# Q and K of batches 2 to 7 loaded four tokens to a partition, and the output weights' sums without one of their waits

## The chip, the cores and the metric

The kernel runs on one core of one Trainium2 chip. The metric is the time of one execution in device microseconds (us). Lower is better. A core has four compute engines, which run their own instruction streams and wait for each other by semaphores: TensorE (PE in the profile; its weight loads are PEld), VectorE (DVE), ScalarE (ACT) and GpSimd (POOL). SyncE (SP) issues transfers here and computes nothing; ACT and POOL issue some as well. All transfers are moved by the same 16 DMA engines of the core.

## What is computed

A block-causal attention over 8 batches of 8 heads, 576 tokens and 64 dimensions, and behind it a layer with a gate:

```
scores = q @ k.T / 8             # per batch and head; a block of 64 tokens sees itself and earlier blocks
attn   = softmax(scores)
x      = (attn @ v), heads side by side      # [4608, 512]
h      = x @ w_in                            # [4608, 2048]
out    = (h / (1 + exp(-beta * h))) @ w_out  # [4608, 512]
```

## The kernel before, in words

The work of attention is cut into 32 units: unit u is the pair of heads c = u % 4 of batch b = u // 4. The rest is cut into 9 chunks of 512 rows of x. All of it is one program on the five instruction streams.

**A unit.** Q and K of two heads are loaded in f32 to ST, cast to bf16 in QKn, transposed on TensorE (a product with the identity, identB) to PSUM, and copied from there to QKT, where a column is a token and the partitions hold the dimensions of two heads. From QKT come the scores (L823, matmuls of 64 rows, two side by side on the array), ScalarE's exponentials E (L844), zeros over what is masked (L850, L852), the product with V (L885), the division (L902, L909), and a transpose of the result (L928) to xT (L939, L941). V is loaded to Vs and cast to Vn (L588), one cast on POOL for a pair of heads.

**Two ways to load Q and K.** For batches 0 and 1 (QB = 2) a load (L710) takes 512 tokens of two heads with four tokens to a partition: 1 KB in a row from memory, 256 KB in all. The last 64 tokens of the batch's 8 heads (the tails) come by four loads of 64 KB (L674), are cast to QKt (L680) and transposed apart (L686, L696). A tile of a pair is four transposes for Q and four for K, each four to a PSUM tile of their own (L730). Their copy to QKT (L738) puts the tokens in order again: it reads the four transposed tiles in turn. For batches 2 to 7 a load (L753) takes all 576 tokens of four heads, 128 to a tile, 576 KB in packets of 256 bytes; four casts (L764) follow, 20 transposes for two units (L775) in PSUM tiles of 7, 7 and 6, and three copies (L785) in order, by VectorE, ScalarE and VectorE.

**A chunk.** For each of 16 pieces of the 2048 columns there are four matmuls (L1121), a tanh on ScalarE (L1131), and a product on VectorE (L1135) to gT. Chunk 0 then multiplies by w_out as it stands (L1157). Chunks 1 to 8 use a scheme of seven block products instead of eight (L1042); it needs sums and differences of quarters of w_out (L986, eight instructions on VectorE, written by `weights()`), and of gT (L1006). The sums TW are kept in OV, a buffer that at first holds V of batch 1; QKt lies in it too. In the kernel before, these sums wait for `wout` (the loads of w_out), for the users of what lay in OV, and for the last product of chunk 0 (`plain[-1:]`). The two that write into w_out itself wait for all of `plain` in any case.

**What sets the order.** A planner (`Plan.schedule`) goes through the operations with given durations, a model of two transfer rings, the number of buffers (slots) and eight PSUM banks. At each moment it starts on a free engine the ready operation with the lowest `prio`. What results is a fixed order for each engine, in which each instruction waits for semaphores on the chip. So an operation that is late on the chip holds all that stands behind it on its engine. `pr(u)` is the due number of a unit's work on TensorE. POOL's numbers are low for casts of Q and K, 4b + 0.5 for V's casts, and 4.6 for the loads of w_out parts 1 to 3 (L511, 512 KB each), which POOL issues; part 0 comes earlier. The loads of Q, K and V are issued by SP in a list's order: Q and K of the units, with the tails behind a batch's first pair, and V behind the fourth or second pair. Until the first 50 us of the plan are over, TensorE fills gaps with products that nobody reads (L447, L535).

Of the kernel before, what the change touches and what calls it, by code (L numbers as in the profile page):

```python
# [359 lines left out]
def bass_blockwise_causal_attn__then__act_swish_beta_kernel(  # L360
# [10 lines left out]
    with es:  # L371
# [1 line left out]
            return es.enter_context(nc.sbuf_tensor(name, shape, dt))  # L373

        NQ = 2
        QB, CAST = 2, "POOL"
        TURN = ((0, 7, "DVE"), (7, 14, "ACT"), (14, 20, "DVE"))
        NE = 3
        PARTS = [((0, 4, "SP", (4, 5, 0, 1, 2, 3)), (4, 8, "SP", range(2)), (4, 8, "POOL", (4, 5, 2, 3)))] + [((0, 8, "SP", range(6)),)] * 7
# [13 lines left out]
        TW = {k: OVh[:, k - 2] for k in (2, 3, 4)}  # L393
        SW = {k: OVh[:, k + 1] for k in (2, 3)}
        QKn = [sb(f"QKn{i}", [128, 2, 1280], bf16) for i in range(NQ)]
        QKt = OV[:, 0:256].bitcast(bf16).rearrange("p (w n) -> p w n", w=2)
        Vn = [sb(f"Vn{i}", [128, 5, 8, 66], bf16) for i in range(NQ)]
        QKT = [sb(f"QKT{i}", [128, 2, 1280], bf16) for i in range(3)]
        Ef = [sb(f"E{i}", [128, 3200], bf16) for i in range(NE)]
# [35 lines left out]
        def act_t(n, ptr=0):  # L435
            return 0.833 * n + 93 + 93 * ptr

        def dve_t(n):
            return (n + 125) / 0.96
# [174 lines left out]
        for u in range(NU):  # L614
# [8 lines left out]
            if b < QB:  # L623

                if c == 0:
                    quads = [(tn, tt_), (P.tile("QKn"), P.tile("QKT"))]
                    tq = P.tile("QKt")
                    early.append(tq)
                    tails = []
                    if b < 1:  # L630
                        tes_ = [P.tile("TT"), P.tile("TT")]
# [5 lines left out]
                        for a in range(2):  # L637
# [3 lines left out]
                            for w, src in enumerate((q, k)):  # L641
                                def fl(g, e, rows=rows, a=a, w=w, src=src):
                                    return [g.dma_start(STt[w][rows], src[0, 4 * a:4 * a + 4, 512:576].rearrange("h t d -> t h d"))]

                                def fn(g, e, rows=rows, w=w):
                                    y, x = QKt[rows, w, :], STt[w][rows].rearrange("p h d -> p (h d)")
                                    return g.activation(y, x, ACT.Copy) if e == "ACT" else g.tensor_copy(y, x)
# [4 lines left out]
                            def ft(g, e, pa=pa, rows=rows):  # L652
                                for i in range(4):
                                    z = g.transpose(PSb[:, pa.slot, 64 * i:64 * i + 64], QKt[rows, i // 2, 128 * (i % 2):128 * (i % 2) + 128], identB[rows, rows])
                                return z
# [46 lines left out]
                    tn, tt_ = quads[c // 2]  # L702
                    tail = tailc[c // 2]
                turned = []
                for w, (nm, src) in enumerate((("Q", q), ("K", k))):
                    ts, pt = P.tile("ST"), P.tile("P1")
                    early6.append(ts)

                    def fl(g, e, ts=ts, src=src, b=b, c=c):
                        return [g.dma_start(STm[ts.slot].rearrange("p h j d -> p h (j d)"),  # L710
                                            src[b, 2 * c:2 * c + 2, 0:512].rearrange("h (p j) d -> p h (j d)", j=4))]

                    o = ld[nm, u] = P.op("SP", 420 if b else 500, fl, tiles=[ts], xfer=750 if b else 820, prio=u, dma=["d_S", 0, 1])
                    o.pkt = 63.0

                    def fn(g, e, ts=ts, tn=tn, p=p, w=w):
                        return g.tensor_copy(QKn[tn.slot][:, p, 640 * w:640 * w + 512].rearrange("p (j h d) -> p j h d", j=4, h=2),
                                             STm[ts.slot].rearrange("p h j d -> p j h d"))

                    onp = u not in (0, 3) or w == 1  # L720
                    o = P.op("POOL" if onp else "DVE", 620 if onp else 430, fn, deps=[o], tiles=[ts, tn],
                             prio=-40 + 3 * u if onp else -1)
                    if u == 0 and w == 1:
                        for x in ones:
                            if x.dur < 160:
                                x.after = o if x.dur > 150 else None

                    def ft(g, e, tn=tn, pt=pt, p=p, w=w):
                        for i in range(4):
                            z = g.transpose(PSb[:, pt.slot, 128 * i:128 * i + 128],  # L730
                                            QKn[tn.slot][:, p, 640 * w + 128 * i:640 * w + 128 * i + 128], identB[:])
                        return z

                    o = P.op("PE", 4 * 56, ft, deps=[o, c4], tiles=[tn, pt, tt_], lat=4 * 56 + 170, mode="full",
                             prio=pr(u))

                    def fc(g, e, pt=pt, td=tt_, p=p, w=w):
                        return g.tensor_copy(QKT[td.slot][:, p, 640 * w:640 * w + 512].rearrange("c (p j) -> c p j", j=4),  # L738
                                             PSb[:, pt.slot, 0:512].rearrange("c (j p) -> c p j", j=4))

                    o.rest = 400.0 if b else 0.0

                    if u in (1, 3):
                        o.after = fqs[u - 1, 0]
                    turned.append(P.op("DVE", dve_t(512) + 30, fc, deps=[o], tiles=[pt, tt_], prio=-5 if b < 1 else .5))
                    turned[-1].after = last0["m"] if b else None
            elif p == 0:

                for w, (nm, src) in enumerate((("Q", q), ("K", k))):
                    ts = P.tile("S4")  # L750

                    def fl(g, e, ts=ts, src=src, b=b, c=c):
                        return [g.dma_start(STh[ts.slot], src[b, 2 * c:2 * c + 4].rearrange("h t d -> (h t) d").rearrange(  # L753
                            "(i p) d -> p i d", p=128))]

                    o = P.op("SP", QKI, fl, deps=[o for t in early6 for o in t.users] if b == QB else [],
                             tiles=[ts], xfer=QKX, prio=u, dma=["d_S4", 0, 1])
                    for i in range(2):
                        ld[nm, u + i] = o
                    for a in range(2):  # L760
                        def fn(g, e, ts=ts, tn=tn, a=a, w=w):
                            x = STh[ts.slot][:, 9 * a:9 * a + 5, :]
                            x = bass.AP(x.tensor, x.offset, [x.ap[0], [64, 5], [256, 2], [1, 64]])
                            return g.tensor_copy(QKn[tn.slot][:, a, 640 * w:640 * w + 640].rearrange("p (t h d) -> p t h d", t=5, h=2), x)  # L764

                        casts.append(P.op(CAST, 740, fn, deps=[o], tiles=[ts, tn], prio=u))

                turned = []
                for n0, n1, eng in TURN:
                    pt = P.tile("P1")  # L770

                    def ft(g, e, tn=tn, pt=pt, n0=n0, n1=n1):
                        x = QKn[tn.slot][:].rearrange("p a n -> p (a n)")
                        for i in range(n0, n1):
                            z = g.transpose(PSb[:, pt.slot, 128 * (i - n0):128 * (i - n0) + 128],  # L775
                                            x[:, 128 * i:128 * i + 128], identB[:])
                        return z

                    n = n1 - n0
                    o = P.op("PE", n * 56, ft, deps=casts, tiles=[tn, pt, tt_], lat=n * 56 + 170, mode="full", prio=pr(u))  # L780

                    def fc(g, e, td=tt_, pt=pt, n0=n0, n1=n1):
                        y = QKT[td.slot][:].rearrange("c a n -> c (a n)")[:, 128 * n0:128 * n1]
                        x = PSb[:, pt.slot, 0:128 * (n1 - n0)]
                        return g.activation(y, x, ACT.Copy) if e == "ACT" else g.tensor_copy(y, x)  # L785

                    turned.append(P.op(eng, act_t(128 * n) if eng == "ACT" else dve_t(128 * n), fc, deps=[o],
                                       tiles=[pt, tt_], prio=.5))
# [188 lines left out]
            return x[:, HJ * a:HJ * a + HJ, 256 * b:256 * b + 256]  # L977

        def weights():
            old = wout + plain[-1:] + [o for t in early for o in t.users]  # L980
            b = [quad(w_out, 0, 0), quad(w_out, 0, 1), quad(w_out, 1, 0), quad(w_out, 1, 1)]
            for k, o, x, y, op in ((3, TW[3], b[3], b[1], ALU.subtract), (2, TW[2], TW[3], b[0], ALU.add),
                                   (4, TW[4], b[2], TW[2], ALU.subtract), (1, b[1], b[1], b[0], ALU.subtract)):
                tw[k] = []
                for n in (slice(0, 4), slice(4, 8)):
                    z = P.op("DVE", dve_t(512), mk(lambda g, o=o, x=x, y=y, n=n, op=op: g.tensor_tensor(  # L986
                        o[:, n], x[:, n], y[:, n], op)), deps=old + (plain if k == 1 else []), prio=0.6)
                    z.same = [tw[q][len(tw[k])] for q in {2: [3], 4: [2]}.get(k, [])]
                    z.deps += z.same + ([tw[3][len(tw[k])]] if k == 1 else [])
                    tw[k].append(z)  # L990
# [260 lines left out]
```

## Time and profile before

| what | value |
|---|---|
| median of 10 runs | 352.73 us (351.41 to 354.05) |
| the profiled execution's own time | 352.78 us |
| its span in the profile | 350.7 us |
| TensorE's granted clock | 1.00 |
| busy: PE, DVE, ACT, POOL | 337.3, 234.5, 232.2, 83.7 us |
| products of x and w_in (L1121), one matmul of 512 columns | 576, 0.216 us apart |
| products with w_out in chunks 1 to 8 (L1042), of 256 columns | 1024, 0.109 us apart |
| transposes of Q and K in batches 2 to 7 (L775) | 240 |
| casts of Q and K in batches 2 to 7 (L764) | 48, 774 ns each |
| casts of V (L588) | 28, 770 ns each |
| loads of w_out (L511), issue to landing | 4, 11.2 us in the median |

The page's busy times count a matmul from its start to its end, while the next has already begun; so the distance of starts in the chain or the timeline, not the mean duration, says what one costs. Unit 8 is the first of batch 2. In the list of groups a line reads: line, engine, operation, out<-in, shapes, count | busy us, mean ns | idle us just before, and who ended it. In a timeline it reads: start, length, engine, line, operation, and in brackets the idle time before it with what ended it.

### The profile page before, as it was taken

What the parts mean: (1) busy time and instruction counts of PE and PEld (TensorE: products, weight loads), DVE (VectorE), ACT (ScalarE), POOL (GpSimd) and SP (SyncE); (2) the same over time, 40 slices, a digit from 0 to 9 for tenths busy, and PEclk for the clock granted to TensorE, in tenths of its full rate; (3) what the DMA queues carried; (4) which work ended last, traced back from release to release, by engine and by line L of the source; (5) the groups of instructions that cost most, each with busy time, mean ns of one, the idle gap of its engine ahead of it and who ended that gap; (6) DMA issues with size and microseconds to landing.
All of it is one profiled execution on the core that took longest, in us unless ns stands there. A gap on an engine that the chain in (4) does not pass through costs nothing.

```text
span 350.7 us, 8036 instructions
## 1 busy us (share of the span) xinstructions
PE 337.3 (96%) x3400; PEld 216.9 (62%) x3322; DVE 234.5 (67%) x488; ACT 232.2 (66%) x362; POOL 83.7 (24%) x131
## 2 busy tenths in 40 slices
PE   8999998999999999999999999999999999999996
PEld 2464465464656667666756676676676666666685
DVE  5667672378889476667857685849565777757742
ACT  3958952868686776876596758676688555545521
POOL 6952531547192034200630026000000000000000
DMA  8999998999999813981199020000000100020023
GB/s 233 244 253 235 204 211 153 255 239 204 203 229 238 153 62 79 227 163 62 33 224 210 3 92 0 32 32 33 30 32 2 62 30 33 0 92 30 0 93 120
DMA packets 113524, 42.30 MB, mean 121 GB/s; under 512 B 96576, under 2 KB 112976, under 8 KB 113488
## 3 DMA queue, kind: packets, MB, share of 16 engines
q1 hardware_dynamic: 98640, 28.78, 40.4%
q0 software_dynamic: 5568, 4.36, 7.9%
q10 hardware_dynamic: 9280, 8.65, 7.3%
q8 instruction: 26, 0.43, 0.5%
q14 instruction: 10, 0.08, 0.1%
HBM read 36.71 MB, written 9.44 MB: 132 GB/s over the span
## 4 chain that ended last, share of the span: by engine, by line
PE 76%; DMA 6%; ACT 5%; SPq 5%; DVE 4%; issue 2%; POOL 1%; POOLq 0%
PE PS L1121 28%; PE PS L1042 27%; PE PS L823 6%; PE PS L885 5%; DMA ST<-in_k_dram 4%; SPq L561 4%; PE PS L1157 3%; PE PS L775 3%; ACT E L844 2%; PE PS L928 2%; DVE gT L1135 2%; DMA ST<-in_q_dram 1%; ACT QKT L785 1%; ACT th L1131 1%; PE PS L447 1%
## 5 line engine op out<-in xcount | busy, mean ns | idle before, releaser
L1131 ACT ACTIVATE th<-PS,beta 128x512 f32<-128x512 f32 x144 | 96.4, 696 | 62.3 <-PE PS L1121 61.9
L1121 PE MATMUL PS<-xT,w_in 128*128 128x512 bf16 x534 | 130.0, 379 | 5.3 <-ACT xT L939 0.9
L1135 DVE SCALAR_TENSOR_TENSOR gT<-th,PS 128x512 f16<-128x512 f32 x144 | 95.7, 683 | 39.8 <-ACT th L1131 38.8
L844 ACT ACTIVATE E<-PS 128x1024 bf16<-128x1024 f32 x93 | 92.1, 1032 | 7.2 <-PE PS L823 6.3
L1121 PEld LDWEIGHTS PS<-xT,w_in 128*128 128x128 bf16 x576 | 53.1, 98 | 54.5 <-DVE gT L1135 2.5
L1042 PE MATMUL PS<-w_out,gT 128*128 128x256 f16 x512 | 63.4, 273 | 0.0
L1042 PEld LDWEIGHTS PS<-w_out,gT 128*128 128x128 f16 x512 | 48.6, 98 | 10.5 <-issue 0.6
L764 POOL CAST QKn<-ST 128x640 bf16<-128x640 f32 x48 | 37.1, 774 | 35.0 <-PE PS L775 21.8
L588 POOL CAST Vn<-Vs 128x640 bf16<-128x640 f32 (+1 forms) x28 | 21.5, 770 | 80.8 <-PE PS L885 66.2
L823 PE MATMUL PS<-QKT 64*64 64x64 bf16 (+4 forms) x328 | 34.0, 295 | 0.3 <-DVE QKT L738 0.3
L885 PEld LDWEIGHTS PS<-Vn,E 128*128 128x128 bf16 x930 | 30.9, 97 | 3.4 <-DVE E L852 0.3
L1042 PE MATMUL PS<-OV 128*128 128x256 f16 x256 | 32.7, 273 | 0.1
L885 PE MATMUL PS<-Vn,E 128*128 128x65 bf16 x930 | 32.0, 193 | 0.0
L1063 ACT ACTIVATE ost<-PS 128x512 f32<-128x512 f32 x32 | 19.6, 613 | 18.6 <-PE PS L1042 18.6
L823 PEld LDWEIGHTS PS<-QKT 64*128 64x128 bf16 (+1 forms) x328 | 13.2, 96 | 26.9 <-issue 8.2
L1042 PEld LDWEIGHTS PS<-OV 128*128 128x128 f16 x256 | 24.2, 98 | 5.9 <-issue 0.6
L909 DVE TENSOR_TENSOR xq<-PS,inv 128x640 bf16<-128x640 f32 x31 | 25.5, 822 | 0.8
L850 DVE MEMSET E<- 64x64 uint32 x62 | 6.9, 112 | 26.8 <-ACT E L844 24.9
L1006 DVE TENSOR_TENSOR OV<-gT 128x1024 f16<-128x1024 f16 x32 | 22.7, 715 | 0.7 <-PE PS L1042 0.4
L785 DVE COPY QKT<-PS 128x896 bf16<-128x896 bf16 (+1 forms) x24 | 13.7, 583 | 10.4 <-PE PS L775 10.2
L775 PE MATMUL PS<-identB,QKn 128*128 128x128 bf16 x240 | 17.1, 219 | 2.4 <-POOL QKn L764 1.4
L785 ACT ACTIVATE QKT<-PS 128x896 bf16<-128x896 bf16 x12 | 11.0, 917 | 10.9 <-PE PS L775 10.9
(80 smaller groups left out, 258.5 us busy)
## 6 DMA issues: line engine op xcount, KB each, us to landing
out_dram<-ost ACTq DMA_DIRECT2D x32, 256.0 KB, 2.3
ST<-in_q_dram SPq DMA_DIRECT2D x12, 576.0 KB, 5.5
ST<-in_k_dram SPq DMA_DIRECT2D x12, 576.0 KB, 7.6
Vs<-in_v_dram SPq DMA_DIRECT2D x24, 256.0 KB, 5.2
ST<-in_q_dram SPq DMA_DIRECT2D x8, 256.0 KB, 5.6
ST<-in_k_dram SPq DMA_DIRECT2D x8, 256.0 KB, 5.8
w_in<-in_moe_w_in_dram POOLq DMA_DIRECT2D x4, 512.0 KB, 11.6
w_out<-in_moe_w_out_dram POOLq DMA_DIRECT2D x4, 512.0 KB, 11.2
```

The source lines that it names most:

```text
L764: return g.tensor_copy(QKn[tn.slot][:, a, 640 * w:640 * w + 640].rearrange("p (t h d) -> p t h d", t=5, h=2), x)
L775: z = g.transpose(PSb[:, pt.slot, 128 * (i - n0):128 * (i - n0) + 128], x[:, 128 * i:128 * i + 128], identB[:])
L785: return g.activation(y, x, ACT.Copy) if e == "ACT" else g.tensor_copy(y, x)
L823: z = g.matmul(o, QKT[tqk.slot][r, uu % 2, 640 + 128 * t + y:640 + 128 * t + m + y], x)
L844: return g.activation(y, x, ACT.Exp, scale=0.125)
L885: z = g.matmul(o, eblk(te, t, i, h), Vn[Tv.slot][:, t, 2 * c + h, 0:65], start=(t == 0), stop=(t == i))
L909: return g.tensor_tensor(xq[xq_(tx)][:].rearrange("p i (h d) -> p h i d", h=2), both(pv, 0, 64), x, ALU.mult)
L1006: return P.op("DVE", dve_t(SZ * HC / 2), mk(lambda g: g.tensor_tensor(fo(), fx(), fy(), op)), deps=deps, tiles=tiles, prio=prio)
L1042: x = g.matmul(PS[:, pw.slot, HM * w:HM * w + HM], fa()[:, j, 128 * w:128 * w + 128], fb()[:, j, :], start=first and (pair or w == 0) and ...
L1121: z = g.matmul(PS[:, ph.slot, :], w_in[:, c, 128 * j:128 * j + 128], xT[:, c, row % RX:row % RX + RC], start=(c == 0), stop=(c == 3))
L1131: return g.activation(th[tt.slot][:], PS[:, ph.slot, :], ACT.Tanh, scale=beta[:, j:j + 1])
L1135: return g.scalar_tensor_tensor(out=gT[tg.slot][:, j, :], in0=th[tt.slot][:], scalar=1.0, in1=PS[:, ph.slot, :], op0=ALU.add, op1=ALU.mult)
```

## The change

QB becomes 8, so that batches 2 to 7 take the first of the two ways as well; the second has no users left. Within it, for batches 2 to 7 alone, the eight transposes of a unit (four of Q, four of K) share one PSUM tile of a whole bank (1024 elements in bf16) and wait for both casts; one copy takes all of them, on VectorE for even c and on ScalarE for odd c; both units of a pair are written together, as their scores are; and their due number is lower by 20. QKt becomes a buffer of its own outside OV, and its users leave the list that the sums wait for. The sums no longer wait for `plain[-1:]`.

```diff
-        QB, CAST = 2, "POOL"
+        QB, CAST = 8, "POOL"
...
-        QKt = OV[:, 0:256].bitcast(bf16).rearrange("p (w n) -> p w n", w=2)
+        QKt = sb("QKt", [128, 2, 256], bf16)
...
                     tq = P.tile("QKt")
-                    early.append(tq)
...
-                for w, (nm, src) in enumerate((("Q", q), ("K", k))):
-                    ts, pt = P.tile("ST"), P.tile("P1")
+                for cc in (c,) if b not in JOIN else (c, c + 1) if p == 0 else ():
+                    cast = []
+                    for w, (nm, src) in enumerate((("Q", q), ("K", k))):
+                        ts, pt = P.tile("ST"), P.tile("P1") if b < 2 or w < 1 else pt
...
+                        if b > 1:
+                            cast.append(o)
+                            if w < 1:
+                                continue
+                        else:
+                            cast = [o]
+
+                        def ft(g, e, tn=tn, pt=pt, p=cc % 2, ws=(w,) if b < 2 else (0, 1)):
+                            for w in ws:
+                                for i in range(4):
+                                    k = 128 * i + 512 * (w - ws[0])
+                                    z = g.transpose(PSb[:, pt.slot, k:k + 128],
+                                                    QKn[tn.slot][:, p, 640 * w + 128 * i:640 * w + 128 * i + 128], identB[:])
+                            return z
+
+                        nt = 4 if b < 2 else 8
+                        o = P.op("PE", nt * 56, ft, deps=[*cast, c4], tiles=[tn, pt, tt_], lat=nt * 56 + 170, mode="full",
+                                 prio=pr(4 * b + cc) - 20 * (b > 1))
...
+                        def fc(g, e, pt=pt, td=tt_, p=cc % 2, w=w, n=1 if b < 2 else 2):
+                            y = QKT[td.slot][:, p, :].rearrange("c (w x) -> c w x", w=2)[:, w + 1 - n:w + 1, 0:512].rearrange("c w (p j) -> c w p j", j=4)
+                            x = PSb[:, pt.slot, 0:512 * n].rearrange("c (w j p) -> c w p j", j=4, w=n)
+                            return g.activation(y, x, ACT.Copy) if e == "ACT" else g.tensor_copy(y, x)
+
+                        turned.append(P.op("ACT" if b > 1 and cc % 2 else "DVE", act_t(1024) if b > 1 and cc % 2 else dve_t(1024) + 150 if b > 1 else dve_t(512) + 30, fc, deps=[o], tiles=[pt, tt_], prio=-5 if b < 1 else .5))
...
-            old = wout + plain[-1:] + [o for t in early for o in t.users]
+            old = wout + [o for t in early for o in t.users]
```

In the changed kernel the lines are 11 further from the score products on: L834 for the scores, L844 becomes L855, L1132 and L1053 for the two products of a chunk, L1168 for chunk 0's product with w_out, L997 for the sums, L718 for the casts, L740 for the transposes, L754 for the copies, L679, L685 and L695 for the tails. The planner makes a new order for every engine. On POOL the loads of w_out parts 1 to 3 stood behind part 0 and the four casts of V of batch 1; now they stand behind part 0, four casts of Q and K and two of tails of batch 2 (units 8 and 9), and the four casts of V, in this order: part 0, Q 8, K 8, tail, V, tail, Q 9, V, K 9, V, V, parts 1 to 3. On VectorE six of the eight sums stand between the first and the second product to gT of chunk 1; before, all eight stood behind the sixteenth and last of these products.

## The prediction

> **What bounds the kernel now.** I read the page's head first, then the chain of waits in order of time, then the timelines of POOL, SP and PE around its largest wait, then the groups by line and form.
>
> ```profile
> span 350.7 us, 8036 instructions
> PE 337.3 (96%) x3400; PEld 216.9 (62%) x3322; DVE 234.5 (67%) x488; ACT 232.2 (66%) x362; POOL 83.7 (24%) x131
> PE 76%; DMA 6%; ACT 5%; SPq 5%; DVE 4%; issue 2%; POOL 1%; POOLq 0%
> ```
>
> TensorE is the bound: busy for 96% of the span, and 76% of the chain. The 6% and 5% of DMA and SP's queue lie in one place, which the chain in order of time shows:
>
> ```profile
> 33.80 1.69 SPq L561
> 35.52 0.89 SPq L564
> 37.76 15.78 DMA ST<-in_k_dram
> 53.59 0.73 POOL QKn L764
> 54.38 0.73 POOL QKn L764
> 55.15 0.95 PE PS L775 x14
> 56.11 0.86 PE PS L1157 x4
> ```
>
> So up to 55 us the kernel hangs on loads, and behind it on TensorE alone. From 64 us on I compared, in the trace, the starts of neighbouring matmuls with their columns at 2.4 per ns; what is lost to waits, switches of tile size aside, is some 4 us in 285. Whatever is saved on TensorE there shortens the run; whatever TensorE loses before 64 us lengthens it, for nothing behind can make it up.
>
> POOL's timeline has the instructions that the change rearranges (start, length, what, the wait before):
>
> ```profile
> 22.86 0.61 POOL L717 CAST QKn<-ST 128x512 bf16<-128x512 f32 x1 [0.59 <-DMA ST<-in_q_dram]
> 25.13 0.61 POOL L717 CAST QKn<-ST 128x512 bf16<-128x512 f32 x1 [1.66 <-DMA ST<-in_k_dram]
> ...
> 39.23 0.74 POOL L511 DMA_DIRECT2D w_out<-in_moe_w_out_dram  x1 [4.81 <-DMA OV<-in_v_dram]
> 39.97 3.08 POOL L588 CAST Vn<-OV 128x640 bf16<-128x640 f32 x4
> 42.99 2.22 POOL L511 DMA_DIRECT2D w_out<-in_moe_w_out_dram  x3
> 45.19 1.53 POOL L764 CAST QKn<-ST 128x640 bf16<-128x640 f32 x2
> 53.59 1.50 POOL L764 CAST QKn<-ST 128x640 bf16<-128x640 f32 x2 [6.87 <-DMA ST<-in_k_dram]
> ```
>
> POOL runs in order: what stands ahead of the three w_out issues delays them.
>
> **Part 1: tiles and transposes.** Batches 2 to 7 need 6 x (32 + 4) = 216 transposes instead of 240. Fourteen in a row take 0.80 us in the chain (at 94.56), 57 ns each, so 24 fewer are worth 24 x 0.057 = **1.4 us of TensorE**, all on the path. Scores, value products and both MLP products stay the same in number.
>
> **Part 2: evictions.** The groups by form give the rates:
>
> ```profile
> L738 DVE COPY QKT<-PS 128x512 bf16<-128x512 bf16 x16 | 10.9, 690 | 3.3 <-PE PS L730 3.1
> L785 DVE COPY QKT<-PS 128x896 bf16<-128x896 bf16 x12 | 7.4, 617 | 3.8 <-PE PS L775 3.8
> L785 ACT ACTIVATE QKT<-PS 128x896 bf16<-128x896 bf16 x12 | 11.0, 917 | 10.9 <-PE PS L775 10.9
> L941 DVE COPY xT<-PS 128x512 bf16<-128x512 bf16 x12 | 5.0, 418 | 0.5 <-PE PS L928 0.4
> ```
>
> The new copies read four tiles in turn (stride 128), as L738 does. Contiguous copies cost 0.52 ns an element more (617 against 418 for 384 more); the stride adds (690 - 418)/512 = 0.53. A strided one of 1024 is then 690 + 512 x 1.05 = 1.23 us (between 2 x 418 and 2 x 690). VectorE: 12 x 1.23 + 12 tails x 0.29 (L696) = 18.2 us, before 12 x 0.617 + 12 x 0.550 = 14.0. ScalarE: no row reads with a stride; 1024 elements take 1.03 us at L844, and with VectorE's ratio 690/418 it would be 1.70; I take 1.03, as the nearest row: 12.4 us for 11.0. Both engines are two thirds busy and the transposes come ahead of other PE work (due times 20 lower): cover of about 2.6 us, eight matmuls of L1042 and eight of L1121 (0.87 + 1.73), stands in the new order between a batch's last transposes and its first scores. Cost 0; without that cover the second copy would show, 1.23 less the 0.55 of before, in each of six batches: 4 us.
>
> The Trainium skill's page "VectorE: DVE Perf Modes", section "What auto-detection actually checks", speaks against this part: a 16-bit copy runs at two elements a cycle only with steps of one. The rows agree (690 against 418); by that rule too the copies lengthen and the sum stays, as long as VectorE has room.
>
> **Part 3: loads.** 24 loads of 576 KB become 48 of 256 KB and 24 of 64 KB; bytes are equal. Packets, by the trace: 55,296 of 256 B at 18 ns, against 12,288 of 1 KB at 47 ns and 6,144 of 256 B, over 16 engines 62 us against 43. From 120 us on DMA is mostly idle and this buys nothing; before that it frees the engines. POOL's casts go from 48 x 0.774 to 48 x 0.615 + 12 x 0.401, 37.1 to 34.3 us; it is idle for three quarters.
>
> **Part 4: POOL's queue, the deciding one.** The new order on POOL is: w_out part 0; casts Q8, K8; tail; V pair 4; tail; Q9; V 5; K9; V 6, V 7; then w_out parts 1 to 3 (Q8 is Q of unit 8, the first of batch 2). Before, these three were issued at 42.99 with only four V casts ahead. Now they stand behind K9's landing, and so do the V casts that the value products of units 5 and 6 need.
> When does K9 land? SP is free of batch 1's V at 37.1. Issues of 256 KB cost 0.51 us there and of 64 KB 0.65 (rows at 16 to 19 us), so Q8, K8, four tails, Q9, K9 go out at 37.1, 37.6, 38.1 to 40.1, 40.7 and 41.25. The nearest row is batch 1's second pair, also behind four tails and also with 512 KB weight loads beside it: issued at 16.43 and 17.08, cast at 22.86 and 25.13, 6.4 and 8.05 us later. By it K9 is cast at 49.3; from below, by the shortest landing of such a load (3.0 us), POOL's own work (39.97 + 4 x 0.66 + 2 x 0.45 + 2 x 0.81) lets it end at 45.1. I take 49.3. After 0.66 and two V casts (1.6) the weight parts are issued from 51.6 (from below 46.7).
> Landing: w_in part 0, issued at 13.92, had landed at 21.3, 7.4 us; w_out part 1 took 9.6 (42.99 to 52.6). The parts follow at 4.1 (w_in) or 3.4 us (w_out: 49.3, 52.6, 56.0, 59.4). The loads beside it are of 1 KB, as with w_in, so part 2 lands at 51.6 + 7.4 + 4.1 = **63.1** (57.5 to 65.3).
> In the new PE order the first product of chunk 1 stands behind four products with part 2: 63.1 + 0.9 = 64.0. Before it started at 62.64, with eight more output products done (1.73) and 0.2 of wait: the same work stood at 60.7. **TensorE loses 64.0 - 60.7 = 3.3 us.** At the upper end it is 5.5; at the lower nothing waits, and the gap before, 1.43 at 55.15 and 0.5 by the w_out wait, is won: -1.9. The loss is shared among waits for V 5, V 6 and parts 1 and 2, about 1.4, 0.6, 0.5 and 0.8 us.
>
> The page "DMA: Bandwidth & Descriptors", section "Latency and other measured facts", says that engines 7 and 15 are usually slower with GpSimd-issued transfers. The trace has such a laggard: 15 of 16 parts of the K load at 37.76 had landed by 47.6, the last at 53.5. Without a laggard K9 would come some 2 us earlier and the loss be near 1.3.
>
> **Part 5: weight sums.** Eight sums (L986, 0.69 to 1.2 us) ran from 93.7 to 106.8, behind the last L1157. Six now stand between the first and second gate product of chunk 1, 5 us of VectorE in one piece behind w_out part 3; behind them wait a PSUM bank and an eviction, and PE has output products and transposes in that time. PE's waits around the old place are 1.6 us. Either end is possible, -1.6 to +1.5. Together with the transposes' waits for banks (L775 on ScalarE, 1.8 us behind 75 us), of which batches with one burst may lose some, I take -0.5 for all behind 64 us.
>
> **Sum.** Against the profiled execution's 352.78 (span 350.7): 3.3 - 1.4 - 0.5 = +1.4, **354.2 us**. The median of the runs is 352.73, the same within 0.05.
>
> **Rivals.** (a) *Faster, about 350.4*: K9 lands by 46 and the weight parts before TensorE asks. For it: 1 KB packets move the same bytes in two thirds of the time, and only one weight part competes until then. Against: the row of batch 1. If nothing waits it is -1.9 - 1.4 - 0.5 = -3.8, 349.0; at the bound of 0.3% 351.7; I name the middle. It decides where part 2 lands before about 60.7. (b) *They cancel, 352.8*: part 2 lands near 61.7, and the loss is 1.9. (c) *Much slower, 358.2*: the strided evictions hold each batch's scores. At ScalarE's upper price, 1.70 for 1.03, it is 0.67 in each of six batches on top of the forecast, 4.0. For it: no row shows that copy. Against: PE's cover of 2.6 us, and both engines' idle third. It decides where the copies begin so late that the chain of two on one engine (2 x 1.23 + 0.29) outlasts the cover.
>
> **Numbers.** Forecast 0.45, (a) 0.27, (b) 0.18, (c) 0.10. A measurement of this kernel tells 0.3% (1.06 us) from no change, so (a) is faster, (b) the same, forecast and (c) slower: 0.27, 0.18, 0.55. The range goes from 349.8, within (a), to 357.4, which is the upper loss (5.5 - 1.4 + 0.5 behind 64 us); it leaves out the far part of (a) and (c). Since cases of both signs weigh, the forecast's own range is 353.9 to 357.4.
>
> **What would show it.** Right: POOL's wait for in_k_dram just ahead of the K cast before the last V casts of batch 1, w_out issued near 51, PE waits for w_out or POOL of 2 us or more between 45 and 66, chunk 1's first gate product near 64. Transposes 216, 57 ns apart. Wrong: w_out issued before 48, or chunk 1 starting before 61; a loss behind 70 us; PE waiting on QKT copies for more than 2 us in all.

## The result, and the profile after

The changed kernel takes 356.3 us (median of 18 runs) against 351.79 (63 runs of the kernel before beside it). The ratio is 1.0119, with a 95% interval from 1.010 to 1.0137: slower by 4.2 us, between 3.5 and 4.8. The profiled execution of the changed kernel took 355.98 us, with a span of 354.1; the one of the kernel before stood 1.0 us above its median in this comparison, so the two profiles lie closer together (3.4 us of span) than the kernels do.

The head of the page after:

```profile
span 354.1 us, 8097 instructions
PE 335.7 (95%) x3378; PEld 216.0 (61%) x3298; DVE 239.8 (68%) x488; ACT 234.4 (66%) x362; POOL 81.8 (23%) x143
PE 74%; DMA 12%; DVE 4%; ACT 4%; issue 3%; POOL 2%; SPq 0%; POOLq 0%
```

TensorE is busy for less time than before (335.7 for 337.3 us) in a longer span. DMA's share of the chain has doubled, and VectorE's stays at 4% though it now stands in other places. The chain in order of time shows which (start, length, what):

```profile
41.65 6.11 DMA ST<-in_q_dram
48.56 0.73 POOL Vn L588
50.02 0.73 POOL Vn L588
52.20 0.73 POOL w_out L511
52.93 15.06 DMA w_out<-in_moe_w_out_dram
68.02 1.76 DVE OV L997 x2
70.90 2.42 DVE OV L997 x3
73.97 0.79 PE PS L834 x12
74.76 0.97 PE PS L1168 x4
```

Before, the load of K for units 8 and 9 led to its casts and the transposes. Now the load of Q9 leads through its cast, K9's cast and three V casts (two of them are shown) to the w_out parts, w_out to the six weight sums, and the sums to a group of scores at 73.97. POOL's timeline has the first half of this:

```profile
40.29 0.74 POOL L511 DMA_DIRECT2D w_out<-in_moe_w_out_dram  x1 [4.49 <-DMA OV<-in_v_dram]
41.02 1.30 POOL L718 CAST QKn<-ST 128x512 bf16<-128x512 f32 x2
...
43.20 0.72 POOL L588 CAST Vn<-OV 128x640 bf16<-128x640 f32 x1
47.28 0.40 POOL L679 CAST QKt<-ST 128x256 bf16<-128x256 f32 x1 [3.36 <-DMA ST<-in_k_dram]
47.88 0.61 POOL L718 CAST QKn<-ST 128x512 bf16<-128x512 f32 x1 [0.20 <-DMA ST<-in_q_dram]
48.56 0.72 POOL L588 CAST Vn<-OV 128x640 bf16<-128x640 f32 x1
49.34 0.61 POOL L718 CAST QKn<-ST 128x512 bf16<-128x512 f32 x1
50.02 1.50 POOL L588 CAST Vn<-OV 128x640 bf16<-128x640 f32 x2
51.47 2.22 POOL L511 DMA_DIRECT2D w_out<-in_moe_w_out_dram  x3
```

The cast of V's second pair (48.56) could have run at 43.9, for its data had been there by 40.3, when the first instruction that waits for the loads of V of batch 1 (w_out part 0) ran. It stands behind the tail of K, which waited 3.36 us for its load. On TensorE's timeline this is the largest wait of the run behind 10 us:

```profile
45.59 1.07 PE L896 MATMUL PS<-Vn,E 128*128 128x65 bf16 x30
49.34 1.07 PE L896 MATMUL PS<-Vn,E 128*128 128x65 bf16 x30 [2.68 <-POOL Vn L588]
...
59.76 1.90 PE L1168 MATMUL PS<-w_out,gT 128*128 128x512 f16 x8 [0.56 <-DMA w_out<-in_moe_w_out_dram]
...
63.97 1.04 PE L1168 MATMUL PS<-w_out,gT 128*128 128x512 f16 x4 [1.50 <-DMA w_out<-in_moe_w_out_dram]
65.06 0.81 PE L1132 MATMUL PS<-xT,w_in 128*128 128x512 bf16 x3
...
73.97 0.79 PE L834 MATMUL PS<-QKT 64*128 64x320 bf16 x12 [1.38 <-DVE gT L1146]
```

Chunk 1's first gate product (65.06) had started at 62.64 before. The last line is a wait that Part 5 of the prediction named and then counted as covered: VectorE ran the six sums from 68.02 to 73.2 with nothing but two 0.11 us memsets between, the eviction of a gate product (L1146) stood behind them at 73.24, and the scores needed the PSUM bank that it frees.

The copies came out as estimated. By line and form (count | busy us, mean ns):

```profile
L754 DVE COPY QKT<-PS 128x1024 bf16<-128x1024 bf16 x12 | 14.5, 1218 | 1.2 <-PE PS L740 1.1
L754 ACT ACTIVATE QKT<-PS 128x1024 bf16<-128x1024 bf16 x12 | 12.3, 1024 | 7.3 <-PE PS L740 7.3
```

### The profile page after: what moved, and what is told of

Its sections match the earlier page's. It is cut to its first block, busy times and chain, and to the rows that moved or that the text cites. A ratio compares the mean times of both kernels' runs of the same rounds, so it can differ in the third digit from the quotient of the medians.

```text
span 354.1 us, 8097 instructions
## 1 busy us (share of the span) xinstructions
PE 335.7 (95%) x3378; PEld 216.0 (61%) x3298; DVE 239.8 (68%) x488; ACT 234.4 (66%) x362; POOL 81.8 (23%) x143
## 3 DMA queue, kind: packets, MB, share of 16 engines
q1 hardware_dynamic: 62544, 28.79, 32.5%
## 4 chain that ended last, share of the span: by engine, by line
PE 74%; DMA 12%; DVE 4%; ACT 4%; issue 3%; POOL 2%; SPq 0%; POOLq 0%
PE PS L1132 29%; PE PS L1053 26%; PE PS L896 6%; PE PS L834 6%; DMA ST<-in_k_dram 4%; DMA w_out<-in_moe_w_out_dram 4%; DMA ST<-in_q_dram 3%; PE PS L740 2%; ACT E L855 2%; PE PS L939 2%; DVE OV L997 1%; PE PS L1168 1%; DVE gT L1146 1%; POOL QKn L718 1%; ACT th L1142 1%
## 5 line engine op out<-in xcount | busy, mean ns | idle before, releaser
L1142 ACT ACTIVATE th<-PS,beta 128x512 f32<-128x512 f32 x144 | 97.4, 697 | 62.0 <-PE PS L1132 61.0
L1132 PE MATMUL PS<-xT,w_in 128*128 128x512 bf16 x536 | 130.6, 379 | 5.5 <-DVE gT L1146 1.8
L1146 DVE SCALAR_TENSOR_TENSOR gT<-th,PS 128x512 f16<-128x512 f32 x144 | 96.2, 683 | 43.2 <-ACT th L1142 42.7
L855 ACT ACTIVATE E<-PS 128x1024 bf16<-128x1024 f32 x93 | 91.9, 1025 | 11.0 <-PE PS L834 8.3
L1132 PEld LDWEIGHTS PS<-xT,w_in 128*128 128x128 bf16 x576 | 53.3, 98 | 55.6 <-DVE gT L1146 2.2
L1053 PE MATMUL PS<-w_out,gT 128*128 128x256 f16 x512 | 64.3, 273 | 0.0
L1053 PEld LDWEIGHTS PS<-w_out,gT 128*128 128x128 f16 x512 | 48.7, 98 | 13.6 <-issue 2.1
L718 POOL CAST QKn<-ST 128x512 bf16<-128x512 f32 x62 | 39.9, 644 | 25.0 <-DMA ST<-in_q_dram 10.6
L588 POOL CAST Vn<-Vs 128x640 bf16<-128x640 f32 (+1 forms) x28 | 20.4, 729 | 101.7 <-PE PS L896 94.3
L834 PE MATMUL PS<-QKT 64*64 64x64 bf16 (+4 forms) x328 | 34.0, 295 | 1.6 <-DVE gT L1146 1.4
L1053 PE MATMUL PS<-OV 128*128 128x256 f16 x256 | 32.7, 273 | 0.0
L834 PEld LDWEIGHTS PS<-QKT 64*128 64x128 bf16 (+1 forms) x328 | 13.2, 96 | 27.9 <-issue 11.0
L754 DVE COPY QKT<-PS 128x512 bf16<-128x512 bf16 (+1 forms) x28 | 25.5, 916 | 5.3 <-PE PS L740 4.9
L1053 PEld LDWEIGHTS PS<-OV 128*128 128x128 f16 x256 | 24.0, 98 | 4.7 <-issue 0.6
L740 PE MATMUL PS<-identB,QKn 128*128 128x128 bf16 x256 | 19.6, 222 | 2.5 <-ACT QKT L754 1.3
L740 PEld LDWEIGHTS PS<-identB,QKn 128*128 128x128 bf16 x256 | 15.9, 99 | 9.7 <-DVE QKn L718 2.9
```

The source lines that it names most:

```text
L740: z = g.transpose(PSb[:, pt.slot, k:k + 128], QKn[tn.slot][:, p, 640 * w + 128 * i:640 * w + 128 * i + 128], identB[:])
L834: z = g.matmul(o, QKT[tqk.slot][r, uu % 2, 640 + 128 * t + y:640 + 128 * t + m + y], x)
L855: return g.activation(y, x, ACT.Exp, scale=0.125)
L1053: x = g.matmul(PS[:, pw.slot, HM * w:HM * w + HM], fa()[:, j, 128 * w:128 * w + 128], fb()[:, j, :], start=first and (pair or w == 0) and ...
L1132: z = g.matmul(PS[:, ph.slot, :], w_in[:, c, 128 * j:128 * j + 128], xT[:, c, row % RX:row % RX + RC], start=(c == 0), stop=(c == 3))
L1142: return g.activation(th[tt.slot][:], PS[:, ph.slot, :], ACT.Tanh, scale=beta[:, j:j + 1])
```

## The experiments

Three theories stood at first. **W**: the loss is POOL's order, V casts and w_out behind the loads of batch 2. **S**: it is the six sums in one piece. **E**: it is the strided copies or the smaller loads. Each experiment was timed in five rounds beside the kernel before; a ratio is always to that kernel, with its 95% interval.

### POOL's order of before (e1_pool_order)

```diff
-                                 prio=-40 + 3 * (4 * b + cc) if onp else -1)
+                                 prio=(4 * b + cc if b > 1 else -40 + 3 * (4 * b + cc)) if onp else -1)
```

The tails' casts get `u + .5` for b > 1 in the same way.

> The changed kernel, but the POOL casts of batches 2 to 7 have the due number 4b + cc (their tails u + 0.5) as casts late in the queue had, so POOL's order around 40 us is the one of the kernel before: w_out part 0, four V casts of batch 1, w_out parts 1 to 3, then the casts Q8, K8, tails, Q9, K9. Tiles, transposes, copies, loads and the weights' sums stay as changed. Theory W (w_out and the V casts come late because they stand behind K9's landing): parts 1 to 3 are issued by 46 us, the waits of TensorE for the V cast (2.7 us) and for w_out (0.6 and 1.5 us) go, chunk 1's first gate product starts at 61 to 62.5 us, and the run is about 3 us shorter than the changed kernel, 352 to 353.5. Rival S (the burst of six weight sums on VectorE costs the time, the early waits are made up): 355.5 to 356.5. Rival E (strided copies or smaller loads cost it): 355.5 to 356.5, and the early waits move to the casts of batch 2.

Measured: 352.08 us, ratio 0.9999 (0.998 to 1.0019). The whole loss is gone. TensorE's timeline of this kernel:

```profile
54.51 1.04 PE L1168 MATMUL PS<-w_out,gT 128*128 128x512 f16 x4 [1.31 <-DMA w_out<-in_moe_w_out_dram]
...
62.55 0.81 PE L1132 MATMUL PS<-xT,w_in 128*128 128x512 bf16 x3
...
67.75 1.04 PE L1132 MATMUL PS<-xT,w_in 128*128 128x512 bf16 x4 [1.83 <-DVE gT L1146]
```

The V wait is gone and chunk 1 starts at 62.55. S and E fall as causes of the loss. (The planner orders TensorE anew as well, in this run and in all others: here 28 of chunk 0's 64 output products stand before chunk 1, in the changed kernel 24. So the comparison is with POOL's order and what the planner makes of it.) But a wait for w_out (1.31) and one for the sums' burst (1.83) stayed, against the expectation that the first would go; together they are more than the 1.9 us that the rest of the change was to win.

### The sums held again (e2_sums_held, e3_pool_order_sums_held, e4_before_sums_free)

```diff
-            old = wout + [o for t in early for o in t.users]
+            old = wout + plain[-1:] + [o for t in early for o in t.users]
```

e2 makes this edit in the changed kernel, e3 in e1. e4 does the reverse in the kernel before: QKt in a buffer of its own, and the sums free.

> The changed kernel with the weights' sums held again behind chunk 0's last product (plain[-1:] back in the list); POOL's order is the changed one. Theory W with the sums as a second, smaller term: only the wait of 1.4 to 1.5 us for a bank held by the burst at 73 us goes, the small waits around 96 to 107 us may return (up to 1 us): 354.5 to 356. Rival S (the sums are the whole loss): 352 to 353. The early waits of TensorE for the V cast and for w_out stay in either case, at 2.7 and 2 us.

> The changed kernel with both of the other two edits: POOL's order of before and the weights' sums held behind chunk 0's last product. What remains of the change is the tiles of four tokens, the 24 fewer transposes, the copies of 1024 and the loads of 256 KB. Theory W plus the sums: both losses go and the 1.4 us of transposes are won: 350.5 to 352, at or below the kernel before. Rival E (the strided copies or the smaller loads cost the time): 354 to 356.

> The kernel before with only the sums' part of the change: QKt in a buffer of its own, and the weights' sums not held behind chunk 0's last product nor behind the tails' users. POOL's order, tiles and loads are those of before. If the burst of six sums in one piece by itself holds a bank for TensorE, a wait of 1 to 1.5 us shows near 70 us and the small waits of before around 96 to 107 us (1 us in all) go: 352 to 353.5. Rival S (the sums are the whole loss): 355 to 356. If the sums find room in VectorE's idle time, as the prediction's -0.5 supposed: 351.5 to 352.5.

Measured: e2 359.63 us, 1.0182 (1.0139 to 1.0225); e3 353.16, 1.0027 (1.0002 to 1.0051); e4 352.19, 0.9996 (0.9976 to 1.0016). Theory S is wrong, and in e2 with the opposite sign: holding the sums costs the changed kernel 0.6% more. No theory had expected e2 above 356 us, nor e3 between 352 and 354. The 1.4 us wait at 73 us goes as expected, but the held sums then stand before the copies of the next tiles. TensorE's timeline of e2:

```profile
103.83 0.62 PE L740 MATMUL PS<-identB,QKn 128*128 128x128 bf16 x8 [0.51 <-ACT QKT L754]
104.92 0.40 PE L685 MATMUL PS<-identB,QKt 128*128 128x128 bf16 x4 [0.47 <-DVE QKT L754]
106.28 1.41 PE L1132 MATMUL PS<-xT,w_in 128*128 128x512 bf16 x3 [0.96 <-DVE QKT L695]
```

That is 1.9 us of waits for copies to QKT, and e3 has the same three (0.51, 0.53, 0.96). Most of the rest of e2's loss is half the granted clock for twice 3.4 us, 3.4 us of work in all. The last section shows the first stretch; the second begins at 106.3, behind the three waits above. The profile of the changed kernel has no such stretch. So each place of the sums has a price: about 1.4 to 1.8 us by the burst, about 2 us in the old place. In the kernel before (e4) freeing them changes nothing that can be measured, and its trace has no wait of more than 0.4 us for the burst.

### V casts or w_out? (e5_v_casts_first, e6_w_out_first)

W names two late things. e5 moves only batch 1's V casts ahead of Q8's cast, e6 only the w_out parts.

```diff
# e5
-                             prio=4 * b + 0.5 - (38.5 - 4.6 * (h0 > 0)) * (b < 1))
+                             prio=-17 if b == 1 else 4 * b + 0.5 - (38.5 - 4.6 * (h0 > 0)) * (b < 1))
# e6
-            wout.append(P.op("POOL", 1000, fwo, xfer=3150, dma=(f"d_wout{a}", 1), prio=-18 if a < 1 else 4.6))
+            wout.append(P.op("POOL", 1000, fwo, xfer=3150, dma=(f"d_wout{a}", 1), prio=-18))
```

> The changed kernel with one due number altered: the V casts of batch 1 stand ahead of Q8's cast on POOL (due -17), so they run from 41 us on as in the kernel before; w_out parts 1 to 3 stay behind K9's cast, issued near 51. It takes the two late things apart. Theory W1 (w_out's lateness alone sets chunk 1's start, and the 2.7 us wait for the V cast only takes part of the same loss): the V wait goes, the waits for w_out parts 1 and 2 grow to 4 to 5 us together, chunk 1 starts at 64 to 65.5 as in the changed kernel, 355 to 356.5. Rival V1 (the V casts' lateness is a loss of its own): 353 to 354, with w_out waits as before at 2 us.

> The changed kernel with the due number of w_out parts 1 to 3 set to that of part 0 (-18): all four parts are issued together at 40 to 43 us; the V casts of batch 1 stay behind K9, later than in the changed kernel. Theory W1 (w_out decides): the waits for w_out go, but the value products of units 5 to 7 wait for V casts at 49 to 52 us and take the loss over, 3 to 5 us; 355 to 357. If the V casts cost nothing by themselves (other products of TensorE fill the place): 352 to 353.5.

Measured: e5 352.19 us, 1.0017 (0.9991 to 1.0042). Theory W1, which asked for 355 us or more, fell: moving the V casts alone gives back 1.0% of the 1.2%, though w_out is issued at 50.63, only 0.84 us earlier than in the changed kernel. TensorE's timeline of e5:

```profile
44.59 1.97 PE L896 MATMUL PS<-Vn,E 128*128 128x65 bf16 x60
...
58.19 1.90 PE L1168 MATMUL PS<-w_out,gT 128*128 128x512 f16 x8 [1.50 <-DMA w_out<-in_moe_w_out_dram]
...
62.77 1.03 PE L1132 MATMUL PS<-xT,w_in 128*128 128x512 bf16 x4
...
66.83 1.04 PE L1168 MATMUL PS<-w_out,gT 128*128 128x512 f16 x4 [1.52 <-DMA w_out<-in_moe_w_out_dram]
```

The value products of two units run through (60 matmuls from 44.59). The waits for w_out are still 3.0 us, where the rival V1 had expected 2, and chunk 1's first gate product again stands just behind a product with part 2, but 2.3 us earlier: part 2 landed at 61.9 for 63.9. So the edit does not part the two things cleanly. The V casts' 1.5 us no longer stand between K9's cast and w_out's issue, and the parts land 1.2 to 2.1 us earlier. The profiled execution took 354.21 us, 2.0 more than the median of e5, so its waits may not be those of most executions. What w_out's late issue costs with the V casts in place is read from the ratios: against e1 0.6 us (1.1 either way), against e7, which differs from e5 in more than that, 1.7 us at most (1.3 either way).

e6: 357.82 us, 1.0177 (1.0145 to 1.021). The waits for w_out go, but the loss is larger than in the changed kernel. POOL's timeline:

```profile
41.09 2.96 POOL L511 DMA_DIRECT2D w_out<-in_moe_w_out_dram  x4 [4.58 <-DMA OV<-in_v_dram]
...
50.01 0.40 POOL L679 CAST QKt<-ST 128x256 bf16<-128x256 f32 x1 [4.20 <-DMA ST<-in_k_dram]
52.17 0.61 POOL L718 CAST QKn<-ST 128x512 bf16<-128x512 f32 x1 [1.76 <-DMA ST<-in_q_dram]
54.34 0.61 POOL L718 CAST QKn<-ST 128x512 bf16<-128x512 f32 x1 [1.55 <-DMA ST<-in_k_dram]
55.01 3.07 POOL L588 CAST Vn<-OV 128x640 bf16<-128x640 f32 x4
```

With four w_out parts in flight K9's cast comes at 54.34 instead of 49.34, and the V casts stand behind it. TensorE waits 3.31 and 3.94 us for POOL, for the tail and for a cast of batch 2, since the planner had put those transposes ahead of the value products. In the same execution half the clock was granted from 49.3 to 59.5 us. So w_out first does not help while the V casts stand behind K9, and it does harm through the loads beside it. Of the two moves, that of the V casts gives far more back; how much of it comes through the earlier landing of w_out, neither run parts.

### Both early (e7_pool_order_w_out_first, e8_w_out_first_sums_spread, e9_two_due_numbers)

e7 is e1 with e6's edit. e8 adds to e7 that each of the first six sums also waits for one of chunk 0's output products (`plain[2]` to `plain[7]`). e9 is the changed kernel with the edits of e5 and e6 alone.

> POOL's order of the kernel before (as in e1_pool_order) with w_out parts 1 to 3 ahead of the V casts instead of behind them: all four issued from 41 us, V casts from 44, then Q8 and so on. In e1_pool_order TensorE waited 1.3 us for part 1 (landed at 53.7) and 1.8 us behind the six sums, which waited 2.3 us for part 3 (landed at 60.5). Parts landing some 3 us earlier should take both away: 1.5 to 3 us off, 349 to 350.5. If instead the V casts (2.2 us later) or K9's landing take their place: 352 or more.

> e7_pool_order_w_out_first with the weights' sums not in one piece: each of the first six is held behind one of chunk 0's output products, one after another, so that VectorE's evictions of gate products come between them. If the sums' burst still holds a bank in e7, this is up to 1.5 us faster than e7; if w_out's earlier landing has already taken that wait away, the same as e7 within 0.7 us.

> The changed kernel with two due numbers altered and nothing else: all four w_out parts at -18 and batch 1's V casts at -17, so both stand ahead of Q8's cast on POOL; the later casts keep the changed due numbers. e5 (V casts first, w_out late) came to 1.0017 of the kernel before, e6 (w_out first, V casts late) to 1.0177, e7 (both early) to 0.9968. If only the place of these two before K9's landing matters: as e7, 349.5 to 351.5, ratio 0.993 to 0.999. If the due numbers of the later batches' casts cost something too: 352 or more.

Measured: e7 350.38 us, 0.9968 (0.9942 to 0.9995); e8 350.69, 0.997 (0.9947 to 0.9994); e9 352.44, 0.9999 (0.997 to 1.0028). In e7 both waits of e1 are gone: TensorE has none for w_out, none over 0.4 us for L1146 between 38 and 80 us, and chunk 1 starts at 61.40. Part 1 landed at 51.10 for 54.46 in e1, part 3 at 58.14 for 61.42 (by the traces; the expectation has e1's some 0.8 us too early). The version is 1.1 us faster than the kernel before (0.2 to 2.0). e8 is the same as e7 within its interval, so no gain is left in the burst that could be measured. e9 has the same order on POOL up to 50 us, and its ratio misses the 0.993 to 0.999 that was expected if this order is all that counts. Its trace has a wait of 1.35 us for a cast and one of 0.84 us behind a tanh (L1142) at 67 to 70 us, where e7 has 0.68 for the cast. But e8 and e12, as fast as e7, wait 1.30 and 1.94 us for a cast there, so that wait does not tell the kernels apart. The intervals of e7 and e9 overlap; whether the later casts' due numbers cost something stays open.

### The tiles and the copies (e10_before_w_out_first, e11_copies_on_vector, e12_copies_on_scalar)

e10 is the kernel before with e6's edit, to weigh the tiles. e11 and e12 are e7 with all 24 copies on one engine (`...` stands for the rest of a line, which stays as it is):

```diff
# e11
-                        turned.append(P.op("ACT" if b > 1 and cc % 2 else "DVE", act_t(1024) if b > 1 and cc % 2 else dve_t(1024) + 150 if b > 1 ...
+                        turned.append(P.op("DVE", dve_t(1024) + 150 if b > 1 ...
# e12
+                        turned.append(P.op("ACT" if b > 1 else "DVE", act_t(1024) if b > 1 ...
```

> The kernel before with only w_out parts 1 to 3 ahead of batch 1's V casts (due -18): tiles, transposes, copies, loads and sums as before. Beside e7 it weighs the tiles of four tokens alone: 24 fewer transposes are 1.4 us by their durations. If that is gained on the path, this kernel is 1 to 2 us slower than e7, 351 to 352.5. If the strided copies or the smaller loads give it back: the same as e7, 350 to 351.

> e7_pool_order_w_out_first with all 24 copies of 1024 on VectorE (1.22 us each by the trace), none on ScalarE. The prediction gave the copies nothing for their cover of 2.6 us and put the price beyond it at two copies and a tail in a row on one engine, 2 x 1.22 + 0.28 = 2.7 us. With cover: 350 to 351.5. Without (rival c): 0.7 to 1.2 us in each of six batches, 354.5 or more.

> e7_pool_order_w_out_first with all 24 copies of 1024 on ScalarE (1.02 us each by the trace), none on VectorE. ScalarE also has the gates' activations, so a copy can stand behind 0.7 to 1 us of other work. With cover: 350 to 352. Without: 354 or more.

Measured: e10 352.87 us, 1.0029 (0.9992 to 1.0067); e11 360.24, 1.0218 (1.0181 to 1.0255); e12 351.54, 0.9972 (0.9949 to 0.9995). e7 over e10 is 0.9968/1.0029 = 0.994, or 2.1 us with some 1.6 either way; the spans differ by 1.7 (348.5 and 350.2). e7 also has the sums free and e10 has them held, so this is the price of tiles and sums together; e4 found nothing for the sums alone. It agrees with 1.4 us of transposes gained where no wait takes them back, without proving the number. e12 is like e7, and e11 costs 2.5% more than e7. Its copies take as long as the others (1207 ns), but four of them and VectorE's other work stand in one row. TensorE's timeline of e11 in one batch:

```profile
174.33 0.62 PE L740 MATMUL PS<-identB,QKn 128*128 128x128 bf16 x8 [0.22 <-DVE QKT L754]
175.54 0.40 PE L685 MATMUL PS<-identB,QKt 128*128 128x128 bf16 x4 [0.59 <-DVE QKT L754]
177.40 0.72 PE L939 MATMUL PS<-identB,xq 128*128 128x128 bf16 x5 [1.46 <-DVE QKT L754]
```

The same waits return at 253 us (0.15, 0.62 and 1.46 us). Behind 40 us TensorE waits 5.2 us for copies to QKT in all, against 1.0 in e7. The waits are not the whole loss: behind those shown, half the clock was granted from 177.0 to 180.4 us, which costs another 1.7 us, and all six executions of e11 have a mean granted clock of 0.99 or 0.995, where e7's twelve have 0.999 or 1.00. With 1.0 us more of waits for casts this accounts for some 7 of the 9.3 us between the two spans; the rest was not traced. So the cover that the prediction counted holds for the split over two engines, and for ScalarE alone, not for VectorE alone.

## Why the prediction was right in its mechanism and short in its size

- **The order on POOL (Part 4), right.** w_out was to be issued from 51.6 and was from 51.47; TensorE's products with part 2 were to start at 63.1 and did at 63.97. Undoing that order (e1) takes the loss away. K9's cast was forecast at 49.3 and ran at 49.34, and that close a hit is luck: its load was issued at 42.30 for 41.25, landed at 48.60 instead of 49.3, and the cast then stood behind Q9's and a V cast on POOL. POOL's long wait (3.36 us) was for the K tail, not for K9 as the prediction's sign had it. The last two of the 16 parts of K9's load landed 0.08 us apart, so there was no laggard, and the loss was still above the 1.3 us that the prediction gave for that case. The 576 KB load of K had one in the profiles of e4 and e10 too (3.5 and 3.7 us behind the fifteenth part); which DMA engine moved that part, no run here shows.
- **The share of the two late things, wrong.** The step took w_out part 2's landing for what sets chunk 1's start, and under that bound gave the wait for V 5 1.4 of 3.3 us. It was 2.68 us. By e5 the V casts' place is worth 1.0% of the 1.2%, by e6 w_out's place alone wins nothing. The bound itself held in e5 too: there part 2 landed at 61.9 and chunk 1 started 0.9 us behind it. What the step did not have is that part 2 would land 2.1 us earlier with the V casts out of the way, of which 0.84 are the earlier issue. It had not asked which wait would stay if one were removed.
- **The size of that term.** Chunk 1 started at 65.06, against the same work at 60.7 before: 4.4 us for 3.3. Of the 1.1 us more, 0.56 are a later start of the whole run: chunk 0's first product stood at 25.25 before and at 25.81 after, in the same order of instructions. In the 14 profiles of this study it lies between 25.10 and 26.15, whichever kernel, so this is a spread between executions.
- **Transposes (Part 1), right.** 24 fewer; e7 against e10 finds 2.1 us (0.5 to 3.7) for the tiles as a whole, the freed sums included, for 1.4 forecast of the transposes.
- **Evictions (Part 2), right in the prices, not quite in the cover.** 1.218 us for 1.23 and 1.024 for 1.03. But behind 40 us TensorE waits 2.5 us in all for copies to QKT, 0.7 before, where the step had cost 0 and the prediction named more than 2 us as a sign of being wrong; in e7 it is 1.0. By the step's own numbers two copies and a tail on one engine (2.75 us) already outlast the cover of 2.6. A large loss by these waits (rival (c)) shows only where all copies are on VectorE (e11).
- **Loads (Part 3), right as far as it went.** SP's queue moves 62,544 packets for 98,640, and the w_out parts land 4.1 us apart beside 1 KB loads, as forecast from w_in. What the step did not know is how lucky the profile before was: w_out part 0, which waits for the loads of V, was issued at 39.23 there, and in the other 13 profiles, with either tiles, between 39.86 and 41.98. In e1 it was 41.20, so that w_out was issued 2 us later than in the profile before and waited for, though POOL's order was the same.
- **Weight sums (Part 5), the mis-sized term behind 64 us.** Forecast -0.5 with ends of -1.6 and +1.5. The profile has +1.4 by the burst and, by the distances of matmuls behind 75 us, some 0.9 less than before elsewhere: about +0.5. The step had named the bank and the eviction that would wait, and then took them as covered. A loss behind 70 us was another of the prediction's signs of being wrong, and it came (1.38 us at 73.97).
- **The sum.** By the profiles: 4.4 - 0.6 (start) - 1.4 + 0.5 = 2.9, and 3.4 with the start, for +1.4 forecast. By the comparisons the loss is 4.2, of which POOL's order is all (1.0119 against 0.9999), and the rest of the change is 0.0 +- 0.7 for a forecast of -1.9. What e1 lost again are the waits of 1.31 and 1.83 us and 2.6 for copies to QKT, for 0.7 before. A loss of 4.2 on 352.73 is 356.9: it lies within 353.9 to 357.4 because the upper end allowed an early loss of 5.5 us; the sum's +1.4 is a third of the loss. Rivals (a) and (b) needed part 2 to land by 60.7 or 61.7, which it did not.

The rule on 16-bit copies from the Trainium skill's page "VectorE: DVE Perf Modes", section "What auto-detection actually checks", that the prediction weighed (two elements a cycle only with steps of one) is in line with 1218 ns for 1024 strided elements: 1.03 ns for each element above 512, against 0.52 contiguous. What e11 paid for is another matter, the chain of copies on one engine and the clock behind it.

## What to carry to other kernels

When a due number moves work up in an engine's queue, list what it now stands ahead of, and ask of each load that it waits for whether something ready stands behind it: here V casts whose data had been there for 8 us waited for a load of the next batch. Where several late things lie in a row, price each by moving it alone, and look at what the move shifts beside it: the one that ends last in the trace (here w_out) need not be the one whose move gives the time back. And copies that cost little split over two engines can cost 2.5% on one of them with the same duration for each copy, part of it by the clock behind the waits.

## What the runs showed of the hardware

**A pause of 2.2 us on TensorE can be followed by half a clock.** In the profile of e2 the granted clock falls behind the wait for w_out that ends at 65.21. By stretches of 1 us (length, PE busy with its count, granted clock, DMA share, GB/s):

```profile
63.00:64.00 1.00, 0.00 (x1) 1.00 1.16 250
64.00:65.00 1.00, 0.00 (x0) 1.00 1.19 239
65.00:66.00 1.00, 0.79 (x3) 0.69 1.17 247
66.00:67.00 1.00, 0.95 (x3) 0.50 1.18 241
67.00:68.00 1.00, 0.83 (x2) 0.50 1.23 254
68.00:69.00 1.00, 1.00 (x4) 0.60 1.19 279
69.00:70.00 1.00, 1.00 (x10) 1.00 1.13 294
```

Half the clock is granted for some 3.4 us, and four products take 1.75 us for 1.04. A longer pause in the same execution, 3.14 us up to 50.15, was followed by none. In e6 two pauses of 3.3 and 3.9 us went with 0.50 from 49.3 to 59.5, three times as long. Shorter waits close together are enough as well: in e2 the clock falls again at 106.3, behind the three of 0.51, 0.47 and 0.96 us, and in e11 at 177.0, within the one of 1.46 us that follows one of 0.59; the same two waits at 254 to 256 us were followed by none. The Trainium skill's page "TensorE: Matmul & The Clock Gate", section "Part 1: The HAM clock gate (the "warmup" mystery)", describes half a clock after an idle window of about 3.4 us, and a window that runs freely. The length of the slow stretch agrees. The pauses do not: the waits of 2.2 us and less are shorter than such a window, and where the clock falls behind them the measurement decides. What makes one place lose clock and another not, no run here shows.

**The changed kernel loses clock in most executions, though its profile shows none.** 16 of its 19 executions have a mean granted clock of 0.985 to 0.995; the profiled one has 1.00. One stretch of 3.4 us at half the clock would make it 0.995. Of the kernel before, 25 of 29 beside e1 to e4 have 0.999 or 1.00, and of e7 all 12. In the changed kernel this costs little (median 356.19 us of ten executions at 0.995, 355.98 of three at 1.00). That it falls behind the pause at 47 us, and that the waits for w_out behind that take it up, is argued from the order, not shown.

**A strided read from PSUM adds nothing on ScalarE.** 1024 elements in four interleaved runs take 1024 ns; contiguous copies of 896 and 512 took 917 and 599 before, which makes 1023 for 1024 (an estimate along that line). On VectorE the stride doubles the cost of an element (1.03 ns against 0.52).
